# Skipping the 24 unused matmuls also at the end of the first of 16 loop steps

## The chip, the core and the metric

The kernel runs on one core of a Trainium2 chip. Its time is the device time of one execution in microseconds (us), and the figure that counts is the median over several executions. Before the change the four executions shown took 659.02, 660.11, 660.36 and 661.85 us; their median is 660.24 us.

The engines that appear below are TensorE (PE; its weight loads are listed apart as PEld), VectorE (DVE), ScalarE (ACT), GpSimd (POOL) and the sync engine (SP), which here only issues DMA transfers.

## What is computed

The reference is one decoding step of a transformer block with two branches that are summed:

```python
xn = _layernorm(x)                                   # x: [2, 1, 512]
q  = (xn @ wq).reshape(B, Sq, H, Dh)...              # 32 heads of 128
scores = einsum("bhqd,bhkd->bhqk", q, k_cache) * Dh ** -0.5
o  = einsum("bhqk,bhkd->bhqd", softmax(scores), v_cache)
out = x + o.reshape(B, Sq, H * Dh) @ wo + relu(xn @ w1) @ w2
```

The caches are `k_cache` and `v_cache` of shape [2, 32, 8192, 128] in bfloat16, 134 MB each. There are 64 pairs of batch and head, and each has one query row. Nearly all of the 280.5 MB that the kernel reads are these two caches, and every element of them is used once.

## The kernel before, in words

The 64 pairs are taken four at a time (`U = 4`), so the loop has `NP = 16` steps. In each step one K tile `ks` and one V tile `vs` of 8.39 MB are read; each fills 128 partitions with 256 blocks of 128 columns. There is one `ks` and one `vs` buffer in SBUF, and no second copy of either.

In a step TensorE does the following, in the order of its program:

- It waits for the K tile (semaphore `dK`) and makes 256 transposes of 128x128 blocks (line 275). They go into four PSUM buffers `tp`, eight blocks to a buffer; ACT and DVE copy each full buffer into SBUF (`kcopies`, line 429), and from the fifth group on a transpose waits for the copy that frees its buffer (line 312).
- It makes 256 score matmuls (line 282), with two short matmuls among them (`turn` and `spread`, lines 294 and 300) that help to spread the maximum for the softmax. DVE reduces the maxima (line 476), and ACT computes the exponentials (line 550).
- It waits for the V tile (`dV`) and makes 256 matmuls with V (line 335), whose sum lands in `ot`. ACT then copies it out (line 561), and before its next copies it loads an activation table again (listed under line 429, 1.28 us).
- In steps 0 to 13 it ends with 24 matmuls of 128x512 into the PSUM bank `ms` (line 346), whose result nobody reads. A register `reg` that starts at 1 and grows by 1 per step decides on them: `If_lt(reg, NP - 1)`.
- `advance` adds to the counting registers, and the loop jumps back to its top.

SP issues the transfers (line 182). The next K tile is issued when the last transpose of the present one is done (semaphore `pT`), since they share the buffer `ks`; the next V tile is issued when the matmuls with V are done (`sW`). So at any time the tile that is moving and at most one more are on the queue. K of steps 0 and 15, and V of steps 1 and 15, are issued as two halves, the others whole.

After the loop TensorE corrects the softmax sums, computes the dense branch (`w1`, `w2`) and the projection by `wo`, whose weights are loaded into the `ks` buffer once the last transposes are done.

Of the kernel before, what the change touches and what calls it, by code (L numbers as in the profile page):

```python
# [18 lines left out]
WARM = 24  # L19
# [4 lines left out]
def kernel(  # L24
# [13 lines left out]
    P = 128  # L38
# [3 lines left out]

    Bsz, Sq, D = A_x.shape
    _, H, Sk, Dh = A_k_cache.shape
    Dff = B_w1.shape[1]
    assert Dh == P and D % P == 0 and Dff % P == 0 and Sk % HP == 0
# [4 lines left out]
    NP = N // U  # L51
# [17 lines left out]
    def sb(shape, dt, name):  # L69
        return ctx.enter_context(nc.sbuf_tensor(name, shape, dt))  # L70

    def ps(shape, dt, name):
        return ctx.enter_context(nc.psum_tensor(name, shape, dt))
# [14 lines left out]
    identb = sb([P, P], bf16, "identb")  # L88
# [41 lines left out]
    ms = ps([P, 512], f32, "ms")  # L130
# [76 lines left out]
    def advance(eng, regs):  # L207
        for r, step in zip(regs, (1, 2, 2) + (NH,) * NH):
            eng.reg_add(r, r, step)
# [34 lines left out]
    def _(pe):  # L244
        pe.wait_ge(sI, 1)
        pe.wait_ge(sV, 5)
        for kt in range(KT):
            i = pe.transpose(tpx[:, kt, :], xn[:, kt, :], identb[0:Bsz, 0:Bsz])
# [3 lines left out]
        for g in range(QG):  # L252
            for kt in range(KT):
                i = pe.matmul(  # L254
                    qp,
                    lhsT=xz[:, kt, Z - g * Bsz:Z - g * Bsz + QG * Bsz],
                    rhs=vs[:, (kt * QG + g) * 512:(kt * QG + g + 1) * 512],
                    start=(g == 0 and kt == 0),
                    stop=(g == QG - 1 and kt == KT - 1),
                )  # L260
        i.then_inc(sQ, 1)
        pe.wait_ge(sV, 7)
        for l in range(QH):
            i = pe.transpose(
                tpq[:, l, :], qs[:, l * Dh:(l + 1) * Dh], identb[0:QG * Bsz, 0:QG * Bsz]
            )
        i.then_inc(sQ, 1)

        def rep(ap, n):
            return ap.rearrange("p (o u) -> p o u", o=1).to_broadcast([P, n, U])  # L270

        def transposes(e):
            for i in range(EG):
                kk = e * EG + i
                t = pe.transpose(tp[e % 4][:, i, :], ks[:, kk * Dh:(kk + 1) * Dh], identb[:])  # L275
            t.then_inc(pT[e % HG], 1)

        def scores(e):
            for i in range(EG):
                kk = e * EG + i  # L280
                n = min(REP, BK - kk % BK)
                t = pe.matmul(  # L282
                    Sc[:, U * kk:U * (kk + n)],
                    lhsT=kT[e][:, i, :],
                    rhs=rep(q4[:], n),
                    start=True,
                    stop=True,
                )
            if e % (NG // 2) == NG // 2 - 1:
                t.then_inc(sS, 1)  # L290

        def turn(i):
            pe.wait_ge(sM, g[i])
            pe.transpose(  # L294
                trp[:, i * P:(i + 1) * P], mcol[:, i:i + 1], identb[:]
            ).then_inc(sT, 1)

        def spread(i):
            pe.wait_ge(sX, g[i])
            pe.matmul(  # L300
                bc[:, i, :], lhsT=onesb[:], rhs=mx[:, i, :], start=True, stop=True
            ).then_inc(sB, 1)

        regs = counters(pe, mybir.EngineType.PE)
        reg, g, h = regs[0], regs[1:3], regs[3:]
        with pe.Fori(16, NL + 1, 16) as n16:
            pe.wait_ge(dK[0], n16)
            for e in range(NG):
                if e == NG // 2:
                    pe.wait_ge(dK[1], n16)  # L310
                if e >= 4:
                    pe.wait_ge(kR[(e - 4) % HG], h[(e - 4) // HG])
                transposes(e)
                if e >= LAG:
                    scores(e - LAG)
            pe.wait_ge(sQ1, reg)
            for e in range(NG - LAG, NG):
                if e >= NG - 4:
                    pe.wait_ge(kR[e % HG], h[e // HG])
                scores(e)  # L320
                if e == TR[0]:
                    turn(0)
                if e == TR[1]:
                    spread(0)
            pe.wait_ge(sO, reg)
            for kk in range(KB):
                i, first = divmod(kk, KB // 2)
                if first == 0:
                    pe.wait_ge(sP, g[i])
                    if i == 0:  # L330
                        turn(1)
                    pe.wait_ge(dV[i], n16)
                if kk == BC:
                    spread(1)
                t = pe.matmul(  # L335
                    oh[:, i, :],
                    lhsT=vs[:, kk * Dh:(kk + 1) * Dh],
                    rhs=rep(prm[:, kk, :], REP),
                    start=(first == 0),
                    stop=(first == KB // 2 - 1),  # L340
                )
                if first == KB // 2 - 1:
                    t.then_inc(sW, 1)
            with pe.If_lt(reg, NP - 1):
                for i in range(WARM):
                    pe.matmul(  # L346
                        ms[:], lhsT=identb[:],
                        rhs=identb[:].rearrange("p (o k) -> p o k", o=1).to_broadcast([P, 4, P]),
                        start=True, stop=True,
                    )  # L350
            advance(pe, regs)

        pe.wait_ge(sI, 2 + U)
# [1 line left out]
        for u in range(U):  # L355
            t = pe.matmul(  # L356
                dbp[:, :, u], lhsT=onesh[:, u, :], rhs=RS[:].rearrange("p i t -> p (i t)"),
                start=True, stop=True,
            )
        t.then_inc(sH, 1)  # L360
        for k in range(KT):
            pe.matmul(
                fin[:, k * Bsz:(k + 1) * Bsz],
                lhsT=xsb[:, k * P:(k + 1) * P],
                rhs=identb[0:Bsz, 0:Bsz],
                start=(k == 0),
                stop=False,
# [3 lines left out]
        for j in range(FJ):  # L371
            for kt in range(KT):
                i = pe.matmul(  # L373
                    hp[:, j, :],
                    lhsT=w1_v[:, kt, j, :],
                    rhs=xz[:, kt, Z:Z + Bsz],
                    start=(kt == 0),
                    stop=(kt == KT - 1),
                )
# [8 lines left out]
        for dq in range(DQ):  # L388
            t = pe.matmul(
                ox.rearrange("p (b j) -> p b j", b=Bsz),  # L390
                lhsT=sel[:, dq, :],
                rhs=Ob[:, :, dq * WJ:(dq + 1) * WJ],
                start=(dq == 0),
                stop=(dq == DQ - 1),
# [198 lines left out]
```

## Time and profile before

| what | value |
|---|---|
| median of four executions | 660.24 us (659.02 to 661.85) |
| time of the profiled execution | 659.66 us |
| its span, first to last instruction | 657.9 us |
| mean granted TensorE clock | 0.965 of full |
| PE busy | 601.7 us (91%) |
| ACT busy, DVE busy | 290.8 us (44%), 261.7 us (40%) |
| read from HBM | 280.50 MB, 426 GB/s over the span |
| 24 unused matmuls, line 346 | 336 recorded, 74.8 us busy as listed |

The page of the profile lists busy time by engine, the span in 40 slices, the DMA queues, and the chain of work that ended last, followed back from the last instruction. The line "PEclk" is the clock that TensorE was granted, in tenths of full speed. Matmuls overlap in the pipeline, so the mean length listed for one (379 ns for a 128x512) is longer than the distance between two (24 of them take 5.18 us in the chain). In a line of the chain the first number is its start and the second its length, both in us. In a table of windows each engine has its busy time and the number of instructions in brackets; the last three columns are the granted clock, the DMA share and GB/s.

### The profile page before, as it was taken

How to read it: one execution, taken by the hardware profiler on the slowest of the kernel's cores; microseconds unless marked ns; L12 is line 12 of the kernel's file. 1: busy time of each engine (PE TensorE's matmuls, PEld its weight loads, DVE VectorE, ACT ScalarE, POOL GpSimd, SP SyncE). 2: the span in 40 equal slices, each digit the busy share in tenths (PEclk: the TensorE clock that was granted, in tenths of full speed). 3: DMA queues.
4: the chain of work that ended last, by engine and by line, in shares of the span. 5: the costliest groups of instructions: out<-in, count | busy, mean ns of one | idle time of the engine just before them, and what ended most of it. 6: DMA issues, size and time to landing. Idle time of an engine off the chain costs nothing.

```text
span 657.9 us, 27600 instructions
## 1 busy us (share of the span) xinstructions
PE 601.7 (91%) x12987; PEld 545.8 (83%) x12987; DVE 261.7 (40%) x503; ACT 290.8 (44%) x532; POOL 7.1 (1%) x30
## 2 busy tenths in 40 slices
PE   1876999999999999999989999998999999999997
PEld 0576897988889798887969888796988889798987
DVE  1440351716235071633507153260715426071631
ACT  1332453636345363644526264353725345372730
POOL 2000000000000000000000000000000000000000
PEclk9997899989899998999999899999989999998996
DMA  9999999999999999999999999999999999999996
GB/s 381 445 440 436 395 430 410 446 446 426 402 446 446 446 426 402 446 446 446 426 402 446 446 446 426 402 446 446 446 426 402 446 446 446 426 402 441 418 429 277
DMA packets 6223, 280.66 MB, mean 427 GB/s; under 512 B 706, under 2 KB 708, under 8 KB 964
## 3 DMA queue, kind: packets, MB, share of 16 engines
q1 hardware_dynamic: 6208, 280.50, 98.9%
q8 instruction: 8, 0.13, 0.1%
q14 instruction: 3, 0.02, 0.0%
q10 hardware_dynamic: 4, 0.00, 0.0%
HBM read 280.50 MB, written 0.00 MB: 426 GB/s over the span
## 4 chain that ended last, share of the span: by engine, by line
PE 69%; DMA 27%; DVE 2%; issue 2%; ACT 0%; SPq 0%; ACTq 0%
PE tp L275 34%; DMA ks<-in_A_k_cache_dram 27%; PE ot L335 14%; PE Sc L282 12%; PE ms L346 6%; DVE mcol L476 2%; PE Sc L400 1%; PE ms L294 1%; PE ms L373 1%; PE ms L300 0%; ACT L429 0%; ACT kT L429 0%; PE Sc L356 0%; SPq L182 0%; SPq L170 0%
## 5 line engine op out<-in xcount | busy, mean ns | idle before, releaser
L429 DVE COPY kT<-tp 128x1024 bf16<-128x1024 bf16 x320 | 209.2, 687 | 248.6 <-PE tp L275 242.9
L275 PEld LDWEIGHTS tp<-identb,ks 128*128 128x128 bf16 x4096 | 229.4, 98 | 15.3 <-DMA ks<-in_A_k_cache_dram 12.1
L429 ACT COPY kT<-tp 128x1024 bf16<-128x1024 bf16 x192 | 188.1, 1014 | 119.7 <-PE tp L275 119.7
L275 PE MATMUL tp<-identb,ks 128*128 128x128 bf16 x4096 | 231.7, 219 | 9.9 <-DMA ks<-in_A_k_cache_dram 8.4
L335 PE MATMUL ot<-prm,vs 128*128 128x64 bf16 x4096 | 142.1, 199 | 2.5 <-issue 2.5
L335 PEld LDWEIGHTS ot<-prm,vs 128*128 128x128 bf16 x4096 | 138.0, 102 | 4.4 <-issue 2.6
L282 PE MATMUL Sc<-q,kT 128*128 128x64 bf16 (+8 forms) x4096 | 133.5, 191 | 4.3 <-issue 4.3
L282 PEld LDWEIGHTS Sc<-q,kT 128*128 128x128 bf16 x4096 | 128.9, 98 | 5.8 <-issue 4.6
L346 PE MATMUL ms<-identb 128*128 128x512 bf16 x336 | 74.8, 379 | 0.0
L476 DVE TENSOR_REDUCE mcol<-Sc 32x1 bf16<-32x128 f32 x128 | 37.1, 289 | 94.0 <-PE Sc L282 92.7
L550 ACT ACTIVATE prm<-Sc,nm 32x128 bf16<-32x128 f32 x128 | 69.0, 539 | 5.4
L545 ACT COPY nm<-ms 128x4 f32<-128x4 f32 x32 | 5.2, 163 | 141.6 <-PE ms L300 141.6
L346 PEld LDWEIGHTS ms<-identb 128*128 128x128 bf16 x336 | 31.8, 98 | 36.4
L561 ACT COPY OTf<-ot 128x8 f32 x16 | 2.7, 166 | 80.9 <-PE ot L335 80.9
L550 ACT ACTIVATION_READ_ACCUMULATOR prm<-Sc,nm x128 | 32.0, 250 | 0.0
L294 PE MATMUL ms<-identb,mcol 128*1 128x128 bf16 x32 | 7.0, 218 | 22.1 <-DVE mcol L476 22.1
L294 PEld LDWEIGHTS ms<-identb,mcol 128*1 128x1 bf16 x32 | 2.5, 79 | 23.9 <-issue 23.1
L429 ACT ACT_TABLE_LOAD x16 | 20.5, 1283 | 3.6 <-issue 3.5
L254 PE MATMUL ot<-vs,xz 128*16 128x512 bf16 x32 | 9.6, 473 | 8.7 <-DMA vs<-in_A_wq_dram 8.7
L254 PEld LDWEIGHTS ot<-vs,xz 128*16 128x16 bf16 x32 | 3.3, 106 | 14.6 <-issue 12.3
L483 DVE TENSOR_REDUCE mx<-ms 1x4 bf16<-1x128 bf16 x32 | 8.9, 279 | 13.8 <-PE ms L294 13.8
L236 POOL COPY q<-qb 128x4 bf16<-128x4 bf16 x16 | 3.0, 187 | 591.3 <-PE Sc L282 571.8
(61 smaller groups left out, 47.0 us busy)
## 6 DMA issues: line engine op xcount, KB each, us to landing
ks<-in_A_k_cache_dram SPq DMA_DIRECT2D x4, 4096.0 KB, 23.5
vs<-in_A_v_cache_dram SPq DMA_DIRECT2D x4, 4096.0 KB, 21.3
vs<-in_A_wq_dram SPq DMA_DIRECT2D x1, 4096.0 KB, 12.3
ks<-in_B_w_dram SPq DMA_DIRECT2D x2, 1792.0 KB, 15.5
ks<-in_A_wo_dram SPq DMA_DIRECT2D x1, 2304.0 KB
ks<-in_A_wo_dram SPq DMA_DIRECT2D x1, 1024.0 KB, 25.1
ks<-in_A_wo_dram SPq DMA_DIRECT2D x1, 512.0 KB, 25.8
ks<-in_A_wo_dram SPq DMA_DIRECT2D x1, 256.0 KB, 26.0
```

The source lines that it names most:

```text
L254: i = pe.matmul(qp, lhsT=xz[:, kt, Z - g * Bsz:Z - g * Bsz + QG * Bsz], rhs=vs[:, (kt * QG + g) * 512:(kt * QG + g + 1) * 512], start=(g = ...
L275: t = pe.transpose(tp[e % 4][:, i, :], ks[:, kk * Dh:(kk + 1) * Dh], identb[:])
L282: t = pe.matmul(Sc[:, U * kk:U * (kk + n)], lhsT=kT[e][:, i, :], rhs=rep(q4[:], n), start=True, stop=True,)
L294: pe.transpose(trp[:, i * P:(i + 1) * P], mcol[:, i:i + 1], identb[:]).then_inc(sT, 1)
L335: t = pe.matmul(oh[:, i, :], lhsT=vs[:, kk * Dh:(kk + 1) * Dh], rhs=rep(prm[:, kk, :], REP), start=(first == 0), stop=(first == KB // 2 - 1),)
L346: pe.matmul(ms[:], lhsT=identb[:], rhs=identb[:].rearrange("p (o k) -> p o k", o=1).to_broadcast([P, 4, P]), start=True, stop=True,)
L373: i = pe.matmul(hp[:, j, :], lhsT=w1_v[:, kt, j, :], rhs=xz[:, kt, Z:Z + Bsz], start=(kt == 0), stop=(kt == KT - 1),)
L400: t = pe.matmul(fin[:, k * Bsz:(k + 1) * Bsz], lhsT=w[:, j, k * P:(k + 1) * P], rhs=x[:, j, :], start=False, stop=(last and k == KT - 1),)
L429: fn(kT[e][:], tp[e % 4][:]).then_inc(kR[e % HG], 1)
L476: m = v.tensor_reduce(out=mcol[own, i:i + 1], in_=S[own, i * KB // 2:(i + 1) * KB // 2, u], axis=AX.X, op=ALU.max,)
L483: v.tensor_reduce(out=mx[:, i, :], in_=trp[:, i * P:(i + 1) * P].rearrange("o (u m) -> o u m", u=U), axis=AX.X, op=ALU.max, negate=True,). ...
L550: x = a.activation(out=prm[own, k, u], in_=S[own, k, u], func=ACTF.Exp, bias=nm[own, i, u:u + 1], scale=1.0, accum_out=RS[own, i, bass.ds( ...
```

## The change

One more branch is put around the 24 matmuls, so that they are left out where `reg` is 1, in the first step. In steps 1 to 13 they are still made, in steps 14 and 15 they are skipped as before. TensorE's program gains one compare-and-branch per step, and no other engine's program changes.

```diff
-            with pe.If_lt(reg, NP - 1):
-                for i in range(WARM):
-                    pe.matmul(
-                        ms[:], lhsT=identb[:],
-                        rhs=identb[:].rearrange("p (o k) -> p o k", o=1).to_broadcast([P, 4, P]),
-                        start=True, stop=True,
-                    )
+            with pe.If_ne(reg, 1):
+                with pe.If_lt(reg, NP - 1):
+                    for i in range(WARM):
+                        pe.matmul(
+                            ms[:], lhsT=identb[:],
+                            rhs=identb[:].rearrange("p (o k) -> p o k", o=1).to_broadcast([P, 4, P]),
+                            start=True, stop=True,
+                        )
             advance(pe, regs)
```

## The prediction

> **What bounds the kernel now.** I read the page first: how full the DMA queues are, what the granted clock does, and who has the shares of the chain. In the first fence, see that the DMA line is full in every slice but the last, and that nearly all of it is queue q1, the caches. The chain gives TensorE 69%, but that alone does not make TensorE the bound: where two paths are almost equally long, the chain names the one that ended later, if only by tenths of a microsecond.
>
> ```profile
> PEclk9997899989899998999999899999989999998996
> DMA  9999999999999999999999999999999999999996
> ...
> q1 hardware_dynamic: 6208, 280.50, 98.9%
> ...
> PE 69%; DMA 27%; DVE 2%; issue 2%; ACT 0%; SPq 0%; ACTq 0%
> ```
>
> Next the chain in order of time, first around the end of step 0, then at two later steps.
>
> ```profile
> 63.35 2.48 issue
> 65.83 4.19 PE ot L335 x84
> 70.02 5.18 PE ms L346 x24
> 75.20 14.29 PE tp L275 x256
> ...
> 204.44 23.76 DMA ks<-in_A_k_cache_dram
> 228.25 14.47 PE tp L275 x256
> ```
>
> The 24 matmuls of step 0 run from 70.02 to 75.20, and the transposes of step 1 follow without a gap. That looks like 5.18 us on the path. So the question is when the K tile of step 1 was there. The issue line of that one transfer answers: 41.43 + 31.4 = 72.8 us.
>
> ```profile
> L182 SPq DMA_DIRECT2D ks<-in_A_k_cache_dram x1: 327/327/327, 41.4 to 41.4; - x1
> ...
> DMA to landing us min/median/max: 31.4/31.4/31.4
> ```
>
> The timeline shows what else happens at that place: the second half of V for step 1 is issued at 70.05, ACT is through with its copy and table load at 71.83, and the K tile of step 2 is issued at 89.52, when the 256 transposes are done.
>
> ```profile
> 70.05 0.33 SPq L182 DMA_DIRECT2D vs<-in_A_v_cache_dram  x1
> 70.14 0.17 ACT L561 COPY OTf<-ot 128x8 f32 x1 [8.74 <-PE ot L335]
> 70.55 1.28 ACT L429 ACT_TABLE_LOAD   x1 [0.25 <-issue]
> ...
> 89.52 0.33 SPq L182 DMA_DIRECT2D ks<-in_A_k_cache_dram  x1
> ```
>
> Last the table of windows, for rate and clock (the column before the DMA share is the clock).
>
> ```profile
> 31.90:34.10 2.20, 0.02 (x1) 0.02 (x2) 0.87 (x2) 0.17 (x1) 0.00 (x0) 1.00 0.34 149
> 34.10:41.40 7.30, 7.30 (x134) 7.30 (x135) 5.66 (x9) 5.70 (x6) 0.00 (x0) 1.00 0.99 431
> 66.33:69.74 3.41, 3.41 (x71) 3.41 (x68) 0.00 (x0) 0.00 (x0) 0.00 (x0) 0.50 0.80 346
> 90.90:576.50 485.60, 461.43 (x10047) 417.57 (x10043) 194.21 (x370) 222.88 (x417) 2.43 (x13) 0.98 1.00 433
> ```
>
> From 90.9 to 576.5 the queues move 433 GB/s at a DMA share of 1.00. A tile of 8.39 MB at that rate takes 19.4 us, a step of two tiles 38.7 us. The trace's landings agree: K tiles land at 189.5, 228.2, 266.9, 305.6 and so on to 576.5, always 38.7 us apart. The K tile issued at 204.44 takes 23.8 us, not 19.4, because V is still moving when it is issued: the next tile is on the queue about 4.4 us before the one ahead has landed. So DMA is the bound from the first microseconds to about 652 us, and TensorE has slack in each step. Only after the last whole K tile (576.5) does TensorE set the pace, for 81.4 us to the end.
>
> **What can be gained at all.** By the trace's packet records there is one place between 2.4 and 652 us where the 16 DMA engines run short for more than 0.2 us: from 89.9 to 90.9, when on average 9.0 of them have a packet in flight. That is 7 engine-microseconds, 0.44 us of the whole queue. It lies right after V of step 1: ten of its sixteen parts land from 90.1 to 90.8, six only from 91.9 to 92.2, and K of step 2, issued at 89.52, brings its first packets 1.4 us later. This gap is all that an earlier step 1 can close.
>
> **The change, part by part.** Sums are in the time of the profiled execution, 659.66 us; the median of the runs is 660.24, 0.58 above it, and I carry the difference over to the median.
>
> - *24 matmuls removed from step 0:* 5.18 us of TensorE, from 70.02 on. K of step 1 lands at 72.8, so the transposes start at about 72.85 and not at 75.20: 2.35 us are left, and 2.83 us become a wait for K.
> - *What ACT owes:* in the one recorded transition without these matmuls that matters (610.4, step 14 to 15), the fifth group of transposes waited 0.75 us for ACT's first copy, which stands behind the table load. Here ACT is free at 71.83, before 72.85: nothing.
> - *Clock after the new wait:* TensorE idles 2.83 us. Two rows are near. From 31.9 to 34.1 it idled 2.2 us before transposes, and the clock stayed at 1.00. From 63.35 to 65.83 it idled 2.48 us, and the window from 66.33 to 69.74 had 0.50. So the loss is between 0 and, if no transpose ever raises the clock, another 14.3 us. As 2.83 us is longer than both idles, I take one stretch of 3.41 us at half clock: 1.7 us. The transposes then end at 72.85 + 14.3 + 1.7 = 88.85 and K of step 2 is issued 0.67 us earlier than at 89.52.
> - *The DMA gap:* with first packets at 88.85 + 1.4 = 90.25 most of the 0.44 us can go, about 0.3. But the six late parts of V never stood still: 92.2 + 19.4 = 111.6, and K of step 2 landed at 111.5. If they set the pace, the gain is 0. I take 0.2 us, between the two ends.
> - *Step 1 after that:* everything on TensorE is 0.67 us earlier, 2.35 us if the clock holds; its V is there at 92.2, before it is used near 98.5. K of step 2 lands near 111.4 and V of step 2 is issued about 5 us ahead of that, so TensorE meets a tile that is not there sooner, and the rest is again 38.7 us a step.
> - *Moved transfers:* only K of step 2 and V of step 2 are issued earlier, on the same SP queue in the same order. V of step 1 is not: it waits for the matmuls with V, which end at 70.02 as before. POOL's copies follow the scores and come earlier with them.
> - *One branch more per step:* the transition at 610.4 took 0.17 us with compare, skip, additions and jump together. So one more costs between 0 and 0.17 us. In steps 0 to 13 it lies under matmuls still queued or the wait for K, at 610.4 under ACT's 0.75 us, and after step 15 it is at most 0.17 us once. I take 0.
>
> Sum: 659.66 - 0.2 = about 659.45, and on the median 660.24 - 0.2 = 660.0 us. In short: the 5.18 us go to a wait for K (2.83), to the clock (1.7) and to slack.
>
> **A rule against it.** The row from 34.10 to 41.40 is nothing but transposes (and the first scores) right behind an idle of 2.2 us, with the clock at 1.00 throughout. The Trainium skill, page "TensorE: Matmul & The Clock Gate", section "Part 4: PE-mode transpose", says that transposes do not count as TensorE activity for the clock in the way that matmuls do. By it the removed matmuls were what kept the clock up, and the sum would be that of the first rival below, near 671 us; by the row it stays at 660.0. I follow the row, which shows that transposes keep the clock, though not that they win it back.
>
> **The rivals.**
>
> - *Slower: the transposes of step 1 run at half clock throughout.* For it: no row shows transposes that start at half clock. Against it: in every step 14.3 us of transposes alone keep 1.00, and the two stretches of half clock in step 0 were ended by other matmuls after 3.4 and 6.8 us. Then they end at 72.85 + 2 x 14.3 = 101.45. It decides once K of step 2 is issued after 92.2 - 1.4 = 90.8, where even the late parts of the queue stand still: 101.45 - 90.8 = 10.65, so 660.24 + 10.65 = 670.9 us. One more half-clock stretch than I took ends at 90.55 and costs nothing to 1.0 us.
> - *The jump back finds code missing.* In step 0 TensorE stood still for 0.93, 3.39 and 2.48 us ("issue" in the chain), each time until 1.3 to 1.5 us after a 16 KB packet of instruction queue q8; the last such packet in the loop runs from 70.51 to 71.52. If the jump waits for it, TensorE goes on at 73.0, 0.15 us after K: nothing. If it needed a fetch of its own after that one (2.48 to 3.39 us more) it would start at 76.4 at worst, K of step 2 would be issued at 90.7, and the time be 660.2 to 661.4. Against it: q8 carries no packet from 72 to 640 us, over 14 jumps back.
> - *Faster: the chain means what it seems to say.* The start of step 1 moves by 2.35 us and all later work with it: 657.9 us (655.1 if K were no limit). Against it: the queues would have to move what they move now in 2.35 us less, and only 0.44 us of them are free.
> - *The change does not do what it says.* The register is 1 in the first step alone, so 336 recorded matmuls become 312; I give this no chance of its own.
>
> **How the numbers follow.** No measurable change by closing or not closing the gap: 0.82. Up to 1 us lost by a second half-clock stretch or a fetch: 0.08, still no measurable change. All transposes cold, or a larger loss of this kind: 0.05. Faster by 2 us or more: 0.05, mostly for the scatter. About 0.3%, 2.0 us, is what a measurement of this kernel can tell from no change. So faster 0.05, same 0.89, slower 0.06, with a hundredth moved to slower for scatter. The likeliest case alone has 659.8 to 660.24 before scatter. The scatter comes from the end: the matmuls with V of step 14 had a stretch of half clock at 602.2 to 605.6 and took 1.5 us longer than those of step 15; the four executions shown spread over 2.8 us, as zero, one or two such stretches would give. With 1.4 us of it to each side the range is 658.6 to 661.4, which takes in the case of up to 1 us lost.
>
> **What would show it.** Right: no line 346 in step 0, TensorE waiting for K until 72.8 and its transposes starting there; a half-clock stretch of 3.4 us around 73 to 77; K of step 2 issued between 87 and 89.5; K tiles of later steps landing within 0.5 us of 189.5, 228.2 and so on, still 38.7 us apart; 24 matmuls fewer. Wrong: a K tile of step 2 issued after 90.8, a clock of 0.5 over most of the transposes, a packet on q8 between 72 and 80, or later landings moved by a microsecond or more. A K of step 1 that lands at another time would move the 2.35, but not the bound.

## The result, and the profile after

The changed kernel is slower: the median of its 52 executions is 661.01 us, that of the kernel before (78 executions) 659.93 us. The ratio is 1.0019, with a 95% interval of 1.0013 to 1.0026, so about 1.25 us were lost (1.08 between the medians). That is under the 0.3% that the prediction took as its bound, but with so many executions it is clear of noise: forecast was no change with a tenth or two gained, and the truth is a small loss. The profiled execution of the changed kernel took 662.18 us; its span is 660.4 us, 2.5 us more than that of the kernel before. This execution is slower than the median of its kernel by 1.2 us, so it shows the loss larger than it usually is.

The page of the changed kernel first. The clock digits at the start of the span are lower, the DMA line is as full as before, and the chain is shared differently: 46% of it are now waits for K tiles, where it was 27%.

```profile
PEclk9986799999999999999989999998999999898997
DMA  9999999999999999999999999999999999999996
...
PE 52%; DMA 46%; DVE 1%; issue 0%; ACT 0%; SPq 0%; ACTq 0%
```

The chain in order of time, from the end of step 0:

```profile
42.67 30.04 DMA ks<-in_A_k_cache_dram
72.71 0.05 issue
72.76 16.89 PE tp L275 x256
89.65 0.02 issue
89.67 24.34 DMA ks<-in_A_k_cache_dram
114.00 0.05 issue
114.05 14.48 PE tp L275 x256
```

The K tile of step 1 lands at 72.71 and the transposes start at 72.76, as forecast. But they take 16.89 us, and before it was 14.29. So the K tile of step 2 is issued at 89.67, no earlier than before (89.52), and it lands at 114.0; before it landed at 111.6.

The timeline of TensorE around this place has the reason (start, length, engine; the bracket is the idle time before):

```profile
65.55 2.71 PE L335 MATMUL ot<-prm,vs 128*128 128x64 bf16 x84 [1.23 <-issue]
72.76 16.88 PE L275 MATMUL tp<-identb,ks 128*128 128x128 bf16 x256 [4.50 <-DMA ks<-in_A_k_cache_dram]
89.47 2.71 PE L282 MATMUL Sc<-q,kT 128*128 128x64 bf16 x82
```

TensorE waited 4.50 us, not 2.83. The windows of the same stretch show the clock (the third column from the right; the DMA share beside it counts a packet where it starts, so in a short stretch it can exceed 1):

```profile
65.54:68.25 2.71, 2.70 (x84) 2.59 (x84) 0.00 (x0) 0.00 (x0) 0.00 (x0) 1.00 1.28 556
68.25:72.76 4.51, 0.01 (x2) 0.01 (x1) 0.00 (x0) 1.45 (x2) 0.00 (x0) 0.81 0.76 323
71.03:77.86 6.83, 5.10 (x49) 5.11 (x50) 2.00 (x3) 2.03 (x2) 0.00 (x0) 0.50 0.92 393
77.86:89.50 11.64, 11.64 (x211) 11.64 (x210) 10.15 (x17) 9.52 (x10) 0.00 (x0) 1.00 1.03 445
90.90:576.50 485.60, 455.42 (x10041) 412.11 (x10038) 194.22 (x370) 222.91 (x417) 2.43 (x13) 0.99 1.00 431
```

The 84 matmuls with V ran at full clock here, 2.71 us and not 4.19, and were done at 68.25, not at 70.02. From 71.03 to 77.86, two stretches of 3.41 us, the clock was 0.50; only 49 transposes fit there. From 90.9 on the DMA queues are full again. The queues do not make up what they lost at 90 us: the K tile of step 14 lands at 578.9, before at 576.5, and the span is longer by just about these 2.4 us.

### The profile page after: what moved, and what is told of

Same layout as the page of the kernel before. It is cut to its first block, busy times and chain, and to the rows that moved or that the text cites. A ratio compares the mean times of both kernels' runs of the same rounds, so it can differ in the third digit from the quotient of the medians.

```text
span 660.4 us, 27567 instructions
## 1 busy us (share of the span) xinstructions
PE 595.3 (90%) x12963; PEld 542.0 (82%) x12963; DVE 261.9 (40%) x503; ACT 290.9 (44%) x532; POOL 7.1 (1%) x30
## 4 chain that ended last, share of the span: by engine, by line
PE 52%; DMA 46%; DVE 1%; issue 0%; ACT 0%; SPq 0%; ACTq 0%
DMA ks<-in_A_k_cache_dram 46%; PE tp L275 34%; PE ot L335 7%; PE Sc L282 6%; PE ms L347 2%; DVE mcol L477 1%; PE Sc L401 1%; PE ms L374 1%; PE ms L294 0%; ACT L430 0%; PE Sc L357 0%; PE ms L300 0%; ACT kT L430 0%; SPq L182 0%; SPq L170 0%
## 5 line engine op out<-in xcount | busy, mean ns | idle before, releaser
L275 PEld LDWEIGHTS tp<-identb,ks 128*128 128x128 bf16 x4096 | 232.8, 99 | 27.6 <-DMA ks<-in_A_k_cache_dram 26.3
L275 PE MATMUL tp<-identb,ks 128*128 128x128 bf16 x4096 | 235.6, 221 | 21.3 <-DMA ks<-in_A_k_cache_dram 20.4
L335 PE MATMUL ot<-prm,vs 128*128 128x64 bf16 x4096 | 136.5, 196 | 1.2 <-issue 1.2
L335 PEld LDWEIGHTS ot<-prm,vs 128*128 128x128 bf16 x4096 | 132.5, 99 | 3.2 <-issue 1.4
L347 PE MATMUL ms<-identb 128*128 128x512 bf16 x312 | 69.4, 379 | 0.0
L347 PEld LDWEIGHTS ms<-identb 128*128 128x128 bf16 x312 | 29.6, 98 | 33.7
```

The lines of the kernel that those rows point to most:

```text
L335: t = pe.matmul(oh[:, i, :], lhsT=vs[:, kk * Dh:(kk + 1) * Dh], rhs=rep(prm[:, kk, :], REP), start=(first == 0), stop=(first == KB // 2 - 1),)
L347: pe.matmul(ms[:], lhsT=identb[:], rhs=identb[:].rearrange("p (o k) -> p o k", o=1).to_broadcast([P, 4, P]), start=True, stop=True,)
```

## The experiments

Three readings were set against each other, later four; the expectations call them theories or rivals by their letters. The block is the 24 unused matmuls. **A, later D:** the block keeps the clock up over the wait for K; without it the transposes are slow, the next K tile is issued too late, and the DMA queues run dry for a moment. **B:** the added branch costs time in every step. **C:** a skipped block costs clock time in whatever step. **E**, added later: any shortening of the block costs in proportion. The ratios are to the kernel before, with 95% intervals.

### The change again, and the branch alone

The changed kernel without an edit:

> The changed kernel again, as a control beside the three others. Theory A (late K tile): without the 24 matmuls TensorE stands idle for 2.8 to 4.5 us until the K tile of step 1 lands at 72.8, its clock is halved for 3.4 to 6.8 us of the transposes, and the K tile of step 2 is issued at 88.8 to 90.5, when the DMA queues are about to run dry: about 1.2 us over the kernel before (ratio 1.002). Rival B (the added branch costs time in each step) and rival C (a skipped block costs the clock, wherever it is) expect the same here; they part in the other runs.

Measured: 1.0014 (1.0001 to 1.0026). The profile:

```profile
72.76 15.88 PE L275 MATMUL tp<-identb,ks 128*128 128x128 bf16 x256 [3.03 <-DMA ks<-in_A_k_cache_dram]
88.68 0.33 SPq L182 DMA_DIRECT2D ks<-in_A_k_cache_dram  x1
```

TensorE waited 3.03 us, the transposes took 15.9 us, and K of step 2, issued at 88.68, landed at 112.8. In this execution the last 84 matmuls with V of step 0 ran at half clock (4.15 us), as in the execution profiled before (4.19 us); so it can be set beside that one, and the account below rests on it.

The branch with a condition that is always true:

```diff
-            with pe.If_ne(reg, 1):
+            with pe.If_ne(reg, 99):
                 with pe.If_lt(reg, NP - 1):
```

> The added branch is there in every step, but its condition is always true, so that the 24 matmuls run in step 0 as before. Theory A: no difference to the kernel before, within 0.05% (0.3 us). Rival B: all of the loss, about +1.2 us. Rival C: no difference.

Measured: 0.9994 (0.9981 to 1.0008). No cost of the branch shows, and B's +1.2 us lies outside the interval; B falls. Its profile also shows an end of step 0 with the block in place and no half clock right before it: the block starts at 68.41, the transposes at 73.6, and K of step 2 is issued at 88.07.

```profile
73.58 14.46 PE L275 MATMUL tp<-identb,ks 128*128 128x128 bf16 x256
88.07 0.33 SPq L182 DMA_DIRECT2D ks<-in_A_k_cache_dram  x1
```

### Half the block kept in step 0

```diff
+            def spare(n):
+                for i in range(n):
+                    pe.matmul(ms[:], ...)
             with pe.If_lt(reg, NP - 1):
-                for i in range(WARM): ...
+                spare(12)
+                with pe.If_ne(reg, 1):
+                    spare(WARM - 12)
```

> 12 of the 24 matmuls are kept in step 0, about 2.6 us of the 2.8 to 4.5 us until the K tile lands. Theory A: TensorE waits under 2 us, the clock mostly holds, the transposes end near 87.2 and the K tile of step 2 is issued 1 to 2 us earlier than in either kernel, so the gap in the queues closes: 0.3 to 1 us under the kernel before. Rival B: as slow as the change, +1.2 us, since the branch is there too. Rival C: between the two, about +0.6 us.

Measured: 0.9995 (0.9975 to 1.0014), median 658.97 us; one execution of twelve at 664.81 makes the interval wide. In the profiled execution (659.40 us) TensorE waited 1.89 us, the transposes took 14.47 us, and K of step 2 was issued at 87.29. It was run twice more:

> The kernel with 12 of the 24 matmuls kept in step 0, again, since one outlier widened its interval. What stands now (theory D): the block keeps the clock up over the wait for the K tile; where the wait is left empty the transposes run at half clock for 3.4 to 6.8 us, the next K tile is issued 1.5 to 3 us late, and the DMA queues run dry; late queues cost the whole kernel. With 12 the wait is mostly filled and the K tile of step 2 is issued near 87.3: at or under the kernel before, 0 to -1 us, and clearly under the change (661.0). Against it (theory E: any shortening in step 0 costs, in proportion): +0.6 us.

Measured: 0.9994 (0.9985 to 1.0002). The timeline of this kernel, same place:

```profile
69.41 2.75 PE L346 MATMUL ms<-identb 128*128 128x512 bf16 x12
72.89 14.47 PE L275 MATMUL tp<-identb,ks 128*128 128x128 bf16 x256 [0.74 <-DMA ks<-in_A_k_cache_dram]
87.20 4.99 PE L282 MATMUL Sc<-q,kT 128*128 128x64 bf16 x158
```

The transposes start as early as in the changed kernel, at 72.89, but at full clock: 14.47 us. K of step 2 is issued at 87.39 and lands 24.2 us later at 111.6, and the K tile of step 14 lands at 576.0.

> 12 of the 24 matmuls in step 0 for the third time, to settle whether it beats the kernel before. Theory D: -0.3 to -0.9 us against the kernel before, and 1 us or more under the change. Theory E (any shortening in step 0 costs in proportion): +0.6 us.

Measured: 0.9998 (0.9987 to 1.0009), the changed kernel beside it 1.0010 (1.0000 to 1.0021):

> The changed kernel beside them on the same chip. Theory D: +0.9 to +1.5 us, K of step 2 issued between 88.6 and 90.5, its last part landed between 112.5 and 114.5, where the twelve have 111.6.

These two profiles say more than the ratios. In this execution of the twelve, step 0 ended early, TensorE waited 3.84 us all the same, the transposes took 16.09 us, and K landed at 113.1. So twelve fill the wait in two of the three profiled executions, not in all. In the changed kernel the wait was 4.48 us, the transposes 16.1 us, K of step 2 was issued at 88.9 and landed at 113.8, as theory D has it; the loss, 0.7 us by the ratio and 0.9 between the medians, is at or just under the low end of what D expected. The twelve, expected 1 us or more under the change, were 1.16 us under it by the medians. Over the three runs the medians of the twelve are 658.97, 659.11 and 659.14 us, of the kernel before 659.92, 659.94 and 659.41. All three intervals include 1, so that the twelve beat the kernel before is likely but not settled; E, which wanted +0.6 us, falls.

18 instead of 12:

> 18 of the 24 matmuls in step 0. They end at about 72.2 to 73.9, just about when the K tile lands. Theory D: no wait of over 0.6 us, no half clock after it, K of step 2 issued at 87.1 to 88.2: 0 to -1 us against the kernel before. Theory E: +0.3 us.

Measured: 1.0002 (0.9988 to 1.0015), median 659.29 beside 659.94. Wait 0.52 us, transposes 14.47 us, K issued at 87.52.

### More than the block

```diff
             with pe.If_lt(reg, NP - 1):
-                for i in range(WARM): ...
+                spare(WARM)
+                with pe.If_eq(reg, 1):
+                    spare(8)
```

> 32 instead of 24 matmuls in step 0, 1.7 us more, so that the K tile of step 2 is issued at about 89.6 to 91.2 without any idle or clock effect. Theory A: the queues run dry for longer, +1 to +1.7 us. Rival C (the clock is the cost): no loss, as TensorE is warmer. Rival B: at most 0.2 us, one branch.

Measured: 1.0033 (1.0018 to 1.0047), that is +2.2 us (1.2 to 3.1). The profile:

```profile
76.54 14.46 PE L275 MATMUL tp<-identb,ks 128*128 128x128 bf16 x256
91.03 0.33 SPq L182 DMA_DIRECT2D ks<-in_A_k_cache_dram  x1
```

The transposes ran at full clock, but K of step 2 was issued at 91.03, and the packets of the sixteen DMA engines show a hole there. Summed over the engines that have no packet in flight, it is 25.3 engine-microseconds from 89.7 to 92.5, against 7.7 from 89.7 to 90.9 in the kernel before. K landed 1.2 us later than there, at 112.8. So a late K tile costs by itself, without half-clock transposes; C, which expected no loss here, falls as a cost of its own. The loss lies above the 1 to 1.7 us that A expected, with an interval that includes 1.7; the profiled execution, 660.62 us, is one of the two fastest of its twelve.

### Feeding the queues early

The change kept, and K of step 2 issued in two halves:

```diff
-    KSPLIT = (0, NP - 1)
+    KSPLIT = (0, 2, NP - 1)
```

> The change is kept, and the K tile of step 2 is issued in two halves, the first after half of the transposes of step 1 (near 81 to 83). The queues then have work long before 90, however late the transposes end. Theory A: the loss is gone, 0.3 to 1 us under the kernel before, and in the profile no gap at 90 us, although the clock is halved after the wait as in the change alone. Rivals B and C: +1.2 us stays.

Measured: 0.9997 (0.9980 to 1.0015). The timeline:

```profile
72.81 16.09 PE L275 MATMUL tp<-identb,ks 128*128 128x128 bf16 x256 [2.95 <-DMA ks<-in_A_k_cache_dram]
...
81.79 7.47 SPq L182 DMA_DIRECT2D ks<-in_A_k_cache_dram  x2
```

The clock was halved after the wait as in the change alone (16.09 us of transposes), but the first half of K was on the queue at 81.8, no hole stands at 90 us, and the K tile of step 14 lands at 576.0, as early as in any kernel here. By the ratio the loss is gone; by the medians (660.18 us, the change beside it 660.88, the kernel before 659.92) most of it. The +1.2 us that C expected to stay is outside the interval. The gain expected beside it does not show. The kernel before with the same split:

> The kernel before with the K tile of step 2 issued in two halves and nothing else changed. Theory A: the gap of 0.44 us near 90 us closes, 0.3 to 1 us under the kernel before, and the same time as the change with that split: with the queues fed early, the 24 matmuls of step 0 do not matter. Rivals B and C: the split does nothing, 0.

Measured: 0.9999 (0.9984 to 1.0014). The hole at 90 is gone, but K of step 2 landed no earlier (its second half at 111.9), and a hole at 167.3 to 168.5 is new: TensorE was ahead in step 3, waited 2.67 us for its K tile, the transposes took 16.09 us, and K of step 4 was issued at 166.75, 1.1 us later than in the kernel before. The expected gain does not show; that the new hole ate it is likely and not shown, since K of step 4 landed at 189.4, as before.

Splitting three tiles was to close that way out too (the diff is `KSPLIT = (0, 2, 3, 4, NP - 1)`), with the change and without it:

> The change, with the K tiles of steps 2, 3 and 4 issued in halves, so that the queues are fed early in all the steps in which TensorE comes out of a wait with a halved clock. Theory D (the change costs only through K tiles that are issued too late): transposes of step 1 still at 15.7 to 16.9 us, no gap at 90 us and none at 129 or 168, and the same time as the kernel before with the same splits, within 0.1%. If the lost clock also costs on another way, +0.8 us or more over that kernel.

> The kernel before with the same three splits. Theory D: as fast as the change with these splits, and within 0.1% of the kernel before (the gap of 0.4 us near 90 closes, halves move slightly slower). Otherwise it is faster than the change with the splits by 0.8 us or more.

Measured: 1.0029 (1.0015 to 1.0043) with the change, 1.0024 (1.0001 to 1.0047) without. Part of D's expectation is met: with the queues fed early the change makes hardly any difference, 0.42 us between the medians, with intervals that overlap almost wholly. The other part is missed: both are slower than the kernel before. In both profiles the first tile that is whole again, that of step 5, finds TensorE waiting 3.91 and 4.15 us for it, the transposes take 15.8 and 17.06 us, and K of step 6 is issued at 244.55 and 245.31, where the kernel before issues it at 242.74. The wait was moved to where nothing covers it. With the change K of step 6 then lands at 268.7 and that of step 14 at 578.6, 1.8 and 2.1 us later than in the kernel before; without it they land at 267.0 and 577.0, only 0.1 and 0.5 us later, so there the rest of the loss is not explained.

### The same block skipped in another step

```diff
-            with pe.If_ne(reg, 1):
+            with pe.If_ne(reg, 6):
                 with pe.If_lt(reg, NP - 1):
```

> The same 24 matmuls are skipped in step 5 instead of step 0. There TensorE also waits about 5 us for its K tile and the clock is halved, but the next K tile is issued 4.4 us before the tile ahead has landed. Theory A (late K tile): a loss of 1.7 to 3.4 us of transposes fits into those 4.4 us, so no difference to the kernel before, within 0.05%. Rival B (the branch): +1.2 us. Rival C (a skipped block costs the clock wherever it is): +1.2 us.

Measured: 1.0042 (1.0022 to 1.0063), the largest loss of all. A had expected none, C a loss. The chain of this kernel:

```profile
242.39 24.16 DMA ks<-in_A_k_cache_dram
266.55 0.05 issue
266.60 17.05 PE tp L275 x256
283.64 0.02 issue
283.66 23.61 DMA ks<-in_A_k_cache_dram
307.27 0.05 issue
```

and its clock:

```profile
265.20:272.00 6.80, 5.40 (x51) 5.41 (x52) 2.07 (x3) 2.09 (x3) 0.00 (x0) 0.50 1.00 434
272.00:283.40 11.40, 11.40 (x207) 11.40 (x205) 9.98 (x16) 9.36 (x10) 0.00 (x0) 1.00 1.02 443
```

TensorE waited 6.37 us, the transposes took 17.05 us, and K of step 7 came at 283.66; it landed at 307.3, 40.7 us behind the tile before it and not 38.7. So the clock is at work in any step (C was right in that), but what it costs goes, by this profile, through the late K tile, as A says: the hole in the packets lies at 283.6 to 286.8, and of the sixteen parts in which K of step 7 lands, one for each DMA engine, fourteen come from 305.0 to 305.7 and two only at 307.2 to 307.3. A's slip was the 4.4 us of lead. The parts of a tile land 1.8 us apart in this kernel, and first packets come about 1 us or more after the issue. By the packets, the first DMA engine was through with V of step 6 at 283.6, just when K was issued, and its first packet of K came at 286.8. Then that one K tile in halves, with the block still skipped in step 5:

```diff
-    KSPLIT = (0, NP - 1)
+    KSPLIT = (0, 7, NP - 1)
```

> The block is skipped in step 5, which alone cost 2.8 us (0.42%), and the K tile of step 7, the one that was issued late behind the half-clock transposes, is issued in two halves, the first after half of them. Theory D: the clock still drops and the transposes of step 6 still take about 17 us, but the queues are not dry near 285, and most of the loss is gone: 0 to +0.8 us. If the loss came from the clock itself on TensorE's path, or from the branch, it stays at +2 to +2.8 us.

Measured: 1.0016 (0.9998 to 1.0034), about +1.1 us where the skip alone cost 2.8. The transposes of step 6 were as slow (17.3 us), no hole is left at 285 (it was 8.0 engine-microseconds), and most of the loss is gone by the middle value; the two intervals overlap, so how much is not settled.

### Taking the wait away without filling it

The change, and K of step 1 in halves (`KSPLIT = (0, 1, NP - 1)`):

> The change with no matmul in the place of the 24, but with the K tile of step 1 issued in two halves, so that its first half has landed by 65 and the transposes start at about 69 to 70 without a wait. Theory D: no half clock at 70 to 77 and K of step 2 issued near 84 to 87, no gap at 90; but TensorE is then several us early in step 2, waits there, and the loss comes back at the K tile of step 3 (a gap near 129), in whole or part: 0 to +1.2 us. Theory E: +1.2 us with the loss in step 1.

Measured: 1.0031 (1.0017 to 1.0045), more than the +1.2 us that was the upper end. The transposes of step 1 start at 67.2 without a wait for K, and no hole stands at 90. But in step 2 TensorE then waited 5.96 us for its K tile, the transposes took 16.06 us, and K of steps 3, 4 and 5 was each issued 0.8 us later than in the kernel before. A hole stands at 207 to 208.8, and the K tile of step 5 landed at 229.3, in the kernel before at 228.2. The loss was moved on; whether it grew is not settled, as the intervals of this kernel and of the change overlap.

### One more execution of the changed kernel

The changed kernel without an edit, one execution alone:

> A second look at the changed kernel in another execution. Theory A: the wait for the K tile of step 1 lasts 2.8 to 4.5 us, one or two stretches of half clock follow it, K of step 2 is issued between 88.8 and 90.5, and DMA engines are short of packets near 90 us.

Measured: 661.75 us. Wait 4.71 us, transposes 16.6 us, K of step 2 issued at 89.59 and landed at 114.5.

### The executions side by side

From the profiles of the kernels that differ only in what stands at the end of step 0 (us; the transposes from the start of the first to the end of the last; "wait" is TensorE's idle time before the transposes of step 1):

| kernel | wait | 256 transposes | K of step 2 issued, landed | K of step 14 landed | span |
|---|---|---|---|---|---|
| before | 0 | 14.5 | 89.5, 111.6 | 576.5 | 657.9 |
| branch alone | 0 | 14.5 | 88.1, 112.1 | 576.5 | 658.2 |
| twelve (first) | 1.89 | 14.5 | 87.3, 111.5 | 576.0 | 657.6 |
| twelve (second) | 0.74 | 14.5 | 87.4, 111.6 | 576.0 | 657.1 |
| eighteen | 0.52 | 14.5 | 87.5, 111.8 | 576.2 | 657.7 |
| twelve (third) | 3.84 | 16.1 | 89.1, 113.1 | 577.6 | 658.6 |
| change (r1) | 3.03 | 15.9 | 88.7, 112.8 | 577.3 | 658.3 |
| change (r16) | 4.48 | 16.1 | 88.9, 113.8 | 578.7 | 659.6 |
| change (first) | 4.50 | 16.9 | 89.7, 114.0 | 578.9 | 660.4 |
| change (r8) | 4.71 | 16.6 | 89.6, 114.5 | 579.2 | 660.0 |
| eight more | 0 | 14.5 | 91.0, 112.8 | 577.6 | 658.8 |

From the landing of step 2 to that of step 14 each of them takes 464.4 to 464.9 us, so what is lost at step 2 is still there at step 14; from there to the end each takes 80.8 to 81.7 us. In all four executions of the changed kernel K of step 2 lands 1.2 to 2.9 us after the 111.6 of the kernel before, and 0.7 to 2.4 us after the 112.1 of the branch alone; their spans are 0.4 to 2.5 us longer than 657.9. The measured loss lies within that.

## Why the prediction was wrong, point by point

**The bound: right.** DMA sets the pace up to the K tile of step 14; where no tile was issued late, K tiles land 38.7 us apart in every kernel here, and the 5.18 us were never to be had.

**24 matmuls removed: right in kind.** The transposes started at 72.76 (forecast 72.85). The wait was 3.0 to 4.7 us, forecast 2.83.

**The clock after the wait: the size near, the time it was set against wrong.** The prediction took one stretch of half clock, 1.7 us, so that K of step 2 would be issued at 88.85, "0.67 us earlier than at 89.52". Measured in the changed kernel were 1.4 to 2.4 us over 14.5, one stretch in two executions and two in the other two, and issue at 88.7 to 89.7. But the 89.52 was the less usual case. In the execution profiled before, the last 84 matmuls with V of step 0 had themselves run at half clock (66.33 to 69.74), so everything after them was late. Where the block of step 0 was left whole and these matmuls ran at full clock, K of step 2 was issued at 88.1 (branch alone), 87.7 and 87.9 (the two kernels that skip in step 5). Against those the change is 0.6 to 2 us late, and not early. One profiled execution was taken for the usual one, though the half clock stood in the prediction's own fence.

**The DMA gap: the step that failed.** The prediction allowed a gain of 0 to 0.44 us, and a loss only from an issue at 90.8 on, since until then the six late parts of V would set the pace. The second profile of the changed kernel, "change (r1)" in the table, tests just that. Its last matmuls with V ran at half clock as in the execution before, K of step 2 was issued at 88.68, 0.84 us earlier than 89.52, and the hole in the packets was smaller, 3.7 engine-microseconds against 7.7. All of this is as the prediction had it, and yet the tile landed 1.2 us later, at 112.8 and not 111.6. The sixteen parts of the tile show how. In the kernel before they land from 110.7 to 111.6; in r1 fifteen land from 110.5 to 111.8 and one at 112.8; in the first profile of the changed kernel twelve land from 111.4 to 111.8, and four from 112.7 to 114.0. By the packet records, joined end to start into sixteen streams, single DMA engines start the tile far later than the rest: in the first profile the first packets come at 90.6 to 91.1 on most, but on one the pause is 3.2 us, and another that was only through at 91.3 still waits 1.2 us. The first packet is slow too, about 3.0 us where 2.42 is usual. A tile has landed when its last part has, so the slowest of the sixteen counts, and not the mean over them, from which the 0.44 us came, nor the six that were late with V. The term should have read about +1.2 and read -0.2.

**The rivals.** "One more half-clock stretch than I took ... costs nothing to 1.0 us" was the nearest to what happened, with the price too low: a second stretch came in two of the four executions, and while a loss of up to 1 us was given a chance of 8%, the median loss lies just above that. Transposes cold throughout did not happen: in the changed kernel the clock was back at 1.00 at 77.86 with nothing but transposes running since 72.76. So the rule of the Trainium skill that was weighed there ("TensorE: Matmul & The Clock Gate", "Part 4: PE-mode transpose") is against the trace: transposes both keep the clock and win it back, after stretches of half clock of 3.4 to 6.8 us. What the block was good for is told better by that page's "Part 1: The HAM clock gate (the "warmup" mystery)", that an idle stretch of about 3.4 us halves the clock; here shorter waits were enough, 2.67 us in the kernel before with K of step 2 split, so that for this kernel the measured waits count and not the 3.4 us. No fetch of code showed: the packet list of q8 has nothing between 71.5 and 650 us. The branch cost nothing that shows, as taken.

**What stays open.** Why single DMA engines start a tile 1 to 3 us after the others when it is issued at about the time they run dry. Later is not simply worse: an issue at 89.5 (the kernel before) landed at 111.6 and one at 91.0 (eight more) at 112.8, with all sixteen parts within 0.9 us of one another, but one at 89.7 in the changed kernel landed at 114.0. That the loss goes through the K tile of step 2 is shown by the twelve and the split, which bring it down, by the eight more, which make it without slow transposes, and by the landings that stay late to step 14; how the engines share it out is not.

## What to carry to other kernels

Before a saving on one engine is written off as slack, ask what its wait will do: here an idle TensorE came back with half its clock, and the slow work behind it was what issues the next transfer. A kernel bound by DMA still loses where the next tile is put on the queue at the last moment, and the loss is that of the slowest part; so it is the time of the issue that has to be protected, with a margin for the spread of the parts. And read the reference execution itself for half-clock stretches before any time of it is used as the usual one.

## What was not expected of the hardware

- Waits of TensorE before the 256 transposes and what these then took: up to 1.89 us of wait, about 14.5 us; 2.67 to 6.37 us, 15.8 to 17.3 us, with no order by the length of the wait. Counting also the waits for the second half of K in step 0, all of 2.47 us and more were followed by half clock in these profiles, those of 2.02 to 2.19 us were not, and one of 1.94 us was (step 2 of the last execution above: transposes of 16.1 us). So the length of the wait alone does not decide near 2 us.
- Each 16 KB packet of instruction queue q8 in step 0 (six between 29.5 and 71.5 us) stands in the stream of another DMA engine, takes 1.0 us, and the data packet beside it is longer by about 0.5 us. In the kernel before just six of the sixteen parts of K of step 1 land late, at 72.4 to 72.8, the other ten at 70.7 to 71.4. This is read from the packets and was not tried by itself.
